# Score products of an attention on 64 by 64 tiles, in a kernel of attention, experts and MLP

## The chip, the core and the metric
The kernel runs on one core of a Trainium2 chip. TensorE (PE) multiplies matrices, and its weight loads (PEld) are listed beside it; VectorE (DVE), ScalarE (ACT) and GpSimd (POOL) work on tiles; SyncE (SP) issues most transfers. The metric is the device time of one execution in microseconds (us), given as the median of several runs.

## What is computed
```python
# q, k, v: (4, 8, 576, 64); p: (4, 8, 32, 64); all float32
def sm_attn(qq, kk, vv):
    s = scale * np.matmul(qq, kk.transpose(0, 1, 3, 2))
    s = s - np.max(s, axis=-1, keepdims=True)
    a = np.exp(s)
    a = a / (np.sum(a, axis=-1, keepdims=True) + 1e-09)
    return np.matmul(a, vv)
p_packed = sm_attn(p, k, v)               # 32 packed queries a head
out = sm_attn(q, p_packed, p_packed)      # 576 tokens attend to the 32 packed rows
...
for e in range(E):                        # _moe_ref: 4 experts, x: (2304, 512)
    h = np.maximum(x @ w1[e], 0.0)        # w1[e]: (512, 1024)
    out += p[:, e:e + 1] * (h @ w2[e])    # w2[e]: (1024, 512)
...
h = x @ w_in                              # _moe2_ref: 512 -> 2048 -> 512
r = np.maximum(h, 0.0)
return ((s * (r * r) + b) @ w_out).astype(np.float32)
```

## The kernel before
The attention works batch by batch (`bi`, four of them). A batch has two groups of four heads (`gi`), and 576 tokens that are cut into two halves of `HT` = 288 (`h`). A head's 64 channels are folded to 32 partitions and two steps `e`, so four heads fill the 128 partitions.

The first score product, `at_s1(bi, gi)` (line 181), multiplies the packed queries of one group, laid out block-diagonally in `pbd` (128 by 128, made by `block_p`), with that group's transposed k (`kqT`, made on VectorE by `trans_kq`, line 152). It makes one PSUM bank a half. `at_exp1` takes the two maxima (L199), the scalar `nm` (L200) and the exponentials (L204). `at_a1t` transposes the result on TensorE in two banks (L216 and L221), `at_pv` (L235) multiplies with v, `at_rs` and `at_pn` (L252 to L272) normalise and write the block-diagonal `sbd`, and `at_pt` (L278) keeps a transposed copy `ptw` that `fold_w1` (L379) multiplies into the experts' first weights. The second score product, `at_s2(bi, gi)` (L289), multiplies `sbd` with the group's transposed q. `at_s2t`, `at_max2`, `at_exp2`, `at_norm2`, `at_a2t` and `at_fin` make the second softmax, and write `a2`, split into a high and a low part.

All these products are plain float32; the trace lists two records for each, with its weight loads beside them. The experts use products of float32r on the split parts: `m1` (L683) makes one block of hidden values, ScalarE writes its high part `hh` (L693) and VectorE its low part `hl` (L694), and `m2` (L711) adds the block into the accumulators. One `m1` and one `m2` are a unit. `advance()` runs `m1` two units ahead of `m2`.

The order of every engine is that of the program (`tc.manual_schedule`). Batch 0 is written out line by line in front of the first unit (the head). Batches 1 to 3 are woven into the units of expert 0: `at(step, fn, ...)` puts an operation in front of unit `step`, and within a step operations run in the order in which they were put there. Batch `n` begins at `s0`, which is 2 for n=1, 16 for n=2 and 32 for n=3. The transpositions of the k of batch n+1 are put at `s0 + 11` to `s0 + 14` of batch n, which is step 16 for the last of batch 2; those of batch 1 at steps 1 and 2. PSUM banks come from `ps_m` (tag "m", two buffers), `ps_h` and, in the head, from the accumulators. Raw k and q share a tag of two buffers ("kq"), transposed k and q another ("kqT").

Of the kernel before, what the change touches and what calls it, by code (L numbers as in the profile page):

```python
# [19 lines left out]
def attention_experts_mlp_kernel(  # L20
# [87 lines left out]
    def load_kq(src, nm, bi, gi):  # L110
        t = att.tile([P, NJ * D], F32, tag="kq", bufs=2, name=f"{nm}{bi}{gi}")
        x = src[bi, 4 * gi : 4 * gi + 4].rearrange("h (r j) d -> (h r) (j d)", j=NJ)
        if bi == 0:
            for c in kq_cuts(nm, bi, gi):
                nc.sync.dma_start(out=t[:, c], in_=x[:, c])
        elif bi % 2 == 0:
            nc.sync.dma_start(out=t, in_=x)
        else:
            for a, z in pairs(bi):
                nc.sync.dma_start(out=t[64 * a : 64 * a + 64], in_=x[64 * z : 64 * z + 64])  # L120
        kq_in[nm, bi, gi] = t

    def load_p(bi):
        x = p[bi].rearrange("(g h) r d -> (h r) g d", g=G)
        t = p_in[:, G * bi : G * bi + G]
        if bi == 0:
            nc.scalar.dma_start(out=t, in_=x)
        elif bi % 2 == 0:
            nc.sync.dma_start(out=t, in_=x)
        else:  # L130
            for a, z in pairs(bi):
                nc.sync.dma_start(out=t[64 * a : 64 * a + 64], in_=x[64 * z : 64 * z + 64])
# [1122 lines left out]
```

## Time and profile before
| | |
|---|---|
| median of 3 runs | 1116.53 us (1115.78 to 1117.95) |
| the profiled execution's own time | 1117.71 us |
| its span, first to last instruction | 1115.9 us |
| TensorE busy | 1097.7 us, 98% |
| VectorE, ScalarE, GpSimd busy | 61%, 36%, 26% |
| first score product, L181, all batches | 64 records, 18.7 us busy |
| second score product, L289 | 64 records, 18.6 us busy |
| fold of w1, L379 | 128 records, 16.0 us busy |

The rows further down are of these views. The stage table gives a stretch, its length, the busy us of PE, PEld, DVE, ACT and POOL (in brackets how many instructions), the granted clock of TensorE as a share of full speed, the share of the DMA engines and GB/s. The chain of waits follows the work that ended last back to what released it. The view in order of time gives start, duration, engine, line, operation, what is written and read, how many instructions were merged, and in brackets how long the engine was idle ahead of it and who released it. Durations of merged matmuls include the pipeline's tail, so a price is better read from start to start.

### The profile page before, as it was taken

Reading aid. Unit: us, or ns where it says so; the run is one execution under the profiler, and the core shown is the slowest. Engines: PE = TensorE matmul, PEld = TensorE weight load, DVE = VectorE, ACT = ScalarE, POOL = GpSimd, SP = SyncE. Lnnn points to the kernel's source line nnn. Section 1 sums busy time; section 2 is a strip of 40 time slices with the busy share of each in tenths; the row PEclk is TensorE's granted clock in tenths of the full one; section 3 lists DMA queues with packets and bytes.
Section 4 is the critical chain, followed back from the end, with each engine's and each line's share of the span. In section 5 each row is a group of like instructions: output and inputs, shape, how many; then the busy total and the mean of one; then the engine's idle time right before and its main releaser. Section 6 shows DMA issues by size and latency. Waiting matters only on the chain.

```text
span 1115.9 us, 18453 instructions
## 1 busy us (share of the span) xinstructions
PE 1097.7 (98%) x7147; PEld 1025.2 (92%) x7147; DVE 685.2 (61%) x1257; ACT 398.9 (36%) x780; POOL 288.9 (26%) x345
## 2 busy tenths in 40 slices
PE   8899999999999999999999999999999999999998
PEld 5788999999999899999999999988999999999996
DVE  6877655467566446556446633569845766675554
ACT  3423222363344343333343322345532332342111
POOL 1421302133322153323263444353211120210000
PEclk9999999999999999999999999999999999999999
DMA  8632331023306685765665641346666565665522
GB/s 260 168 97 65 82 84 58 21 85 97 125 1 198 234 228 148 215 231 162 213 204 153 172 124 67 130 163 229 269 227 208 173 219 183 208 201 191 191 107 85
DMA packets 68999, 175.08 MB, mean 157 GB/s; under 512 B 11440, under 2 KB 28080, under 8 KB 68912
## 3 DMA queue, kind: packets, MB, share of 16 engines
q1 hardware_dynamic: 68064, 172.79, 48.4%
q8 instruction: 56, 0.92, 0.3%
q10 hardware_dynamic: 848, 1.11, 0.3%
q14 instruction: 31, 0.25, 0.1%
HBM read 127.44 MB, written 46.44 MB: 156 GB/s over the span
## 4 chain that ended last, share of the span: by engine, by line
PE 91%; DVE 4%; POOL 1%; issue 1%; DMA 1%; ACT 1%; DVEq 0%; POOLq 0%; ACTq 0%
PE acc L711 35%; PE h L683 18%; PE o L869 17%; PE h L835 15%; PE s L289 1%; PE pp L478 1%; PE s L181 1%; PE pw L379 1%; PE pp L524 1%; PE pv L235 1%; DMA k<-in_k_dram 1%; DVE gg L803 0%; POOL w2l L549 0%; POOL x L737 0%; DVE qT L152 0%
## 5 line engine op out<-in xcount | busy, mean ns | idle before, releaser
L711 PE MATMUL acc<-hl,w2h 128*128 128x288 f32 x1024 | 303.2, 296 | 0.0
L711 PE MATMUL acc<-hh,w2l 128*128 128x288 f32 x1024 | 302.5, 295 | 0.2 <-POOL w2l L549 0.2
L711 PE MATMUL acc<-hh,w2h 128*128 128x288 f32 x1024 | 302.6, 296 | 0.0
L683 PE MATMUL h<-a,w1p 128*128 128x288 f32 x1536 | 252.0, 299 | 2.1 <-DVE hl L694 0.9
L694 DVE SCALAR_TENSOR_TENSOR hl<-h,hh 128x288 fp32r<-128x288 f32 x256 | 116.2, 454 | 189.6 <-ACT hh L693 188.3
L683 PEld LDWEIGHTS h<-a,w1p 128*128 128x128 f32 x1536 | 217.5, 188 | 14.4 <-issue 9.0
L869 PE MATMUL o<-wo,gg 128*128 128x512 f32 x864 | 224.0, 393 | 3.5 <-DVE gg L803 1.9
L835 PE MATMUL h<-xs,wop 128*128 128x384 f32 x1008 | 204.0, 338 | 0.7 <-DVE y L726 0.7
L835 PEld LDWEIGHTS h<-xs,wop 128*128 128x128 f32 x1008 | 180.7, 188 | 13.8 <-DVE y L726 1.4
L711 PEld LDWEIGHTS acc<-hh,w2l 128*128 128x128 f32 x1024 | 192.3, 188 | 0.6 <-POOL w2l L549 0.4
L711 PEld LDWEIGHTS acc<-hl,w2h 128*128 128x128 f32 x1024 | 192.9, 188 | 0.0
L711 PEld LDWEIGHTS acc<-hh,w2h 128*128 128x128 f32 x1024 | 192.7, 188 | 0.0
L869 PEld LDWEIGHTS o<-wo,gg 128*128 128x128 f32 x864 | 160.9, 188 | 27.8 <-DVE gg L803 2.3
L693 ACT ACTIVATE hh<-h 128x288 fp32r<-128x288 f32 x256 | 104.5, 408 | 221.2 <-PE h L683 218.1
L737 POOL TENSOR_TENSOR x<-x,y 128x288 f32<-128x288 f32 (+2 forms) x144 | 88.4, 649 | 161.9 <-DVE y L726 161.7
L789 ACT ACTIVATE yy<-yy 128x768 f32<-128x768 f32 x48 | 40.2, 838 | 113.0 <-DVE yy L855 113.0
L855 DVE TENSOR_TENSOR yy<-h,uv 128x384 f32<-128x384 f32 x96 | 51.1, 553 | 47.5 <-PE h L835 47.4
L549 POOL TENSOR_TENSOR w2l<-w2r,w2h 128x512 fp32r<-128x512 f32 x32 | 41.5, 1298 | 74.8 <-ACT w2h L548 73.2
L799 ACT ACTIVATE gg<-yy,b_sb 128x768 fp32r<-128x768 f32 x48 | 44.8, 934 | 37.3 <-DVE yy L792 36.0
L803 DVE SCALAR_TENSOR_TENSOR gg<-yy,b_sb,gg 128x768 fp32r<-128x768 f32 x48 | 55.7, 1161 | 1.7 <-ACT gg L799 1.7
L792 DVE SCALAR_TENSOR_TENSOR yy<-yy,s_sb 128x768 f32<-128x768 f32 x48 | 51.2, 1068 | 0.0
L660 POOL TENSOR_TENSOR wo<-wo 128x512 fp32r<-128x512 f32 x16 | 23.9, 1502 | 103.7 <-ACT wo L659 103.7
(370 smaller groups left out, 1028.8 us busy)
## 6 DMA issues: line engine op xcount, KB each, us to landing
xs<-xs_dram SPq DMA_DIRECT2D x63, 768.0 KB, 4.3
w1p_dram<-w1o SPq DMA_DIRECT2D x32, 512.0 KB, 3.8
w1p<-w1p_dram SPq DMA_DIRECT2D x128, 128.0 KB, 4.5
xs_dram<-xs SPq DMA_DIRECT2D x21, 768.0 KB, 3.3
w2r<-in_moe_w_dram SPq DMA_DIRECT2D x32, 256.0 KB, 4.1
w1r<-in_moe_w_dram SPq DMA_DIRECT2D x12, 512.0 KB, 4.8
pb<-pn_dram SPq DMA_DIRECT2D x16, 288.0 KB, 4.4
out_dram<-o_sb SPq DMA_DIRECT2D x17, 256.0 KB, 2.0
```

The lines of the kernel that those rows point to most:

```text
L549: nc.gpsimd.tensor_tensor(out=lo, in0=raw, in1=f32(hi), op=ALU.subtract)
L683: nc.tensor.matmul(t[:, :HT], lhsT=w1p_block(e, bi, f, gi, w), rhs=a2[bi][:, x, gi, tok], start=(n == 0), stop=(n == 3 * G - 1),)
L693: nc.scalar.activation(xh, t[:, :HT], AF.Relu)
L694: nc.vector.scalar_tensor_tensor(out=xl, in0=t[:, :HT], scalar=0.0, in1=f32(xh), op0=ALU.max, op1=ALU.subtract)
L711: nc.tensor.matmul(acc[m][:, :HT], lhsT=w[:, col], rhs=x, start=(f == 0 and n == 0), stop=(f == NF - 1 and n == 2),)
L737: nc.gpsimd.tensor_tensor(out=dst, in0=dst, in1=y[:, a - t0 : z - t0], op=ALU.add)
L792: nc.vector.scalar_tensor_tensor(out=y, in0=y, scalar=s_sb, in1=y, op0=ALU.mult, op1=ALU.mult)
L799: nc.scalar.activation(t[:, 0], y, AF.Identity, bias=b_sb)
L803: nc.vector.scalar_tensor_tensor(out=t[:, 1], in0=y, scalar=b_sb, in1=f32(t[:, 0]), op0=ALU.add, op1=ALU.subtract)
L835: nc.tensor.matmul(ps, lhsT=w[:, a, col], rhs=x[:, z, m, :], start=(n == 0), stop=(n == 3 * HK - 1),)
L855: nc.vector.tensor_tensor(out=dst, in0=ps, in1=src, op=ALU.add)
L869: nc.tensor.matmul(o_acc[i], lhsT=lhsT, rhs=w, start=(f == 0 and n == 0), stop=(f == FG - 1 and n == 2),)
```

## The change
Both score products are cut into 64 by 64 tiles. A tile holds two heads, and a call makes one token half `h` for both groups: `at_s1(bi, h)` issues eight products (two `e`, two groups `g`, two head pairs `c`), with `c` choosing the rows and the PSUM bank and `g` the columns and the half of the output's partitions. From there on the first softmax works by head pairs `c` that hold both groups. `at_s2(bi, h)` does the same, with the groups on the rows and the pairs on the output's halves; q is loaded by pairs to match (`load_q`), and the second softmax works by token halves.

The two maxima of a half are taken in a new `at_max1` behind each product. In batches 1 to 3 ScalarE copies the first half's scores to SBUF there, and the exponential reads that copy. In batch 0 a half is a set of nine of every eighteen tokens, so that it needs only the first or the second part of k. `at_exp1` of the second pair moves from step `s0 + 1` to `s0 + 2`. `pbd` and `sbd` shrink to 64 columns, the zeroing of `sbd` goes, and its transposition is one instruction instead of two. Raw k and q have four buffers instead of two; the first loads of k alternate between the groups, the second v is loaded ahead of q. Lines of the weave that put the transpositions of k are not changed. The core of the diff (renamings in the second softmax are left out):

```diff
+    def load_k(bi, gi, cuts=None):
+        if ("k", bi, gi) not in kq_in:
+            kq_in["k", bi, gi] = att.tile([P, NJ * D], F32, tag="kq", bufs=4, name=f"k{bi}{gi}")
+        x = k_src[bi, 4 * gi : 4 * gi + 4].rearrange("h (r j) d -> (h r) (j d)", j=NJ)
+        for c in [slice(None)] if cuts is None else kq_cuts("k", bi)[cuts]:
+            nc.sync.dma_start(out=kq_in["k", bi, gi][:, c], in_=x[:, c])
+    def load_q(bi, c):
+        t = kq_in["q", bi, c] = att.tile([P, NJ * D], F32, tag="kq", bufs=4, name=f"q{bi}{c}")
+        for g in range(G):
+            h = 4 * g + 2 * c
+            nc.sync.dma_start(
+                out=t[64 * g : 64 * g + 64],
+                in_=q_src[bi, h : h + 2].rearrange("h (r j) d -> (h r) (j d)", j=NJ),
+            )
...
-        t = att.tile([P, G, 2, P], F32, tag="pbd", bufs=2, name=f"pbd{bi}")
+        t = att.tile([P, G, 2, 64], F32, tag="pbd", bufs=2, name=f"pbd{bi}")
...
-    def at_s1(bi, gi, tags="mm"):
-        kt = kqT.pop(("k", bi, gi))
-        ps = []
-        for h in range(2):
-            t = bank(f"s1_{bi}{gi}{h}", tags[h])
-            for e in range(2):
-                nc.tensor.matmul(
-                    t[:, :HT],
-                    lhsT=pbd[bi][:, gi, e, :],
-                    rhs=kt[:, e, h * HT : (h + 1) * HT],
-                    start=(e == 0),
-                    stop=(e == 1),
-                )
-            ps.append(t)
-        stt["s1", bi, gi] = ps
-    def at_exp1(bi, gi):
-        ps = stt.pop(("s1", bi, gi))
-        m2 = att.tile([P, 2], F32, tag="m2", bufs=2, name=f"m2_{bi}{gi}")
-        nm = att.tile([P, 1], F32, tag="nm", bufs=2, name=f"nm_{bi}{gi}")
-        s2 = att.tile([P, 2], F32, tag="s2", bufs=2, name=f"s2_{bi}{gi}")
-        rs = att.tile([P, 1], F32, tag="rs", bufs=2, name=f"rs_{bi}{gi}")
-        a1 = att.tile([P, S], F32, tag="a1", bufs=2, name=f"a1_{bi}{gi}")
-        for h in range(2):
-            nc.vector.reduce_max(m2[:, h : h + 1], ps[h][:, :HT], axis=AX.X)
+    def half(x):
+        return slice(64 * x, 64 * x + 64)
+    def at_s1(bi, h, tags="mm"):
+        ps = stt["s1", bi, h] = [bank(f"s1_{bi}{h}{c}", tags[c]) for c in range(2)]
+        for e in range(2):
+            for g in range(G):
+                for c in range(2):
+                    x = kqT["k", bi, g][half(c), e]
+                    t = ps[c][half(g), :HT]
+                    if bi == 0:
+                        x = x.rearrange("a (r j) -> a r j", j=NJ)[:, :, blocks((h,))[0]]
+                        t = t.rearrange("a (r j) -> a r j", r=32)
+                    else:
+                        x = x[:, h * HT : (h + 1) * HT]
+                    nc.tensor.matmul(
+                        t, lhsT=pbd[bi][half(c), g, e, :], rhs=x, start=(e == 0), stop=(e == 1)
+                    )
+    def at_max1(bi, h):
+        for c in range(2):
+            if h == 0:
+                m2 = att.tile([P, 2], F32, tag="m2", bufs=2, name=f"m2_{bi}{c}")
+                a1 = att.tile([P, S], F32, tag="a1", bufs=2, name=f"a1_{bi}{c}")
+                stt["a1", bi, c] = a1, m2
+            a1, m2 = stt["a1", bi, c]
+            ps = stt["s1", bi, h][c][:, :HT]
+            nc.vector.reduce_max(m2[:, h : h + 1], ps, axis=AX.X)
+            if bi and h == 0:
+                nc.scalar.activation(a1[:, :HT], ps, AF.Copy)
+    def at_exp1(bi, c):
+        a1, m2 = stt["a1", bi, c]
+        nm = att.tile([P, 1], F32, tag="nm", bufs=2, name=f"nm_{bi}{c}")
+        s2 = att.tile([P, 2], F32, tag="s2", bufs=2, name=f"s2_{bi}{c}")
+        rs = att.tile([P, 1], F32, tag="rs", bufs=2, name=f"rs_{bi}{c}")
         nc.vector.scalar_tensor_tensor(
             out=nm, in0=m2[:, 0:1], scalar=m2[:, 1:2], in1=nscale, op0=ALU.max, op1=ALU.mult
         )
         for h in range(2):
+            src = stt["s1", bi, h][c][:, :HT]
+            dst = a1[:, h * HT : (h + 1) * HT]
+            if bi == 0:
+                src = src.rearrange("a (r j) -> a r j", r=32)
+                dst = a1.rearrange("a (r j) -> a r j", j=NJ)[:, :, blocks((h,))[0]]
+            elif h == 0:
+                src = dst
             nc.scalar.activation(
-                a1[:, h * HT : (h + 1) * HT], ps[h][:, :HT], AF.Exp,
-                bias=nm, scale=scale, accum_out=s2[:, h : h + 1],
+                dst, src, AF.Exp, bias=nm, scale=scale, accum_out=s2[:, h : h + 1]
             )
-        stt["a1", bi, gi] = (a1, s2, rs)
+        stt["a1", bi, c] = (a1, s2, rs)
...
-        at, vt = stt["a1t", bi, gi], v_in[bi, gi]
+        at = stt["a1t", bi, gi]
...
-                    rhs=vt[:n, z : z + 2, c, :],
+                    rhs=v_in[bi, x][:n, 2 * gi : 2 * gi + 2, c, :],
...
-        sb = att.tile([P, 2, P], F32, tag="sbd", bufs=2, name=f"sbd_{bi}{gi}")
+        sb = att.tile([P, 2, 64], F32, tag="sbd", bufs=2, name=f"sbd_{bi}{gi}")
         nc.gpsimd.memset(pw, 0.0)
-        nc.gpsimd.memset(sb, 0.0)
         stt["pw", bi, gi], stt["sbd", bi, gi] = pw, sb
...
-        pwf = pw.rearrange("a e d -> a (e d)")
-        for c in range(2):
-            r = slice(64 * c, 64 * c + 64)
-            nc.vector.transpose(
-                out=sb[r, :, r].rearrange("a f (e i) -> a e f i", e=2), in_=pwf[r]
-            )
+        nc.vector.transpose(
+            out=sb.rearrange("a f (e i) -> a e f i", e=2), in_=pw.rearrange("a e d -> a (e d)")
+        )
...
-    def at_s2(bi, gi, hs=(0, 1), tag="m"):
-        if 0 in hs:
-            stt["sc", bi, gi] = att.tile([P, NJ, 32], F32, tag="t", bufs=3, name=f"sc_{bi}{gi}")
-        qt, sb = kqT["q", bi, gi], stt["sbd", bi, gi]
-        for h in hs:
-            t = bank(f"s2_{bi}{gi}{h}", tag)
-            for e in range(2):
-                nc.tensor.matmul(
-                    t[:, :HT],
-                    lhsT=sb[:, e, :],
-                    rhs=qt[:, e, h * HT : (h + 1) * HT],
-                    start=(e == 0),
-                    stop=(e == 1),
-                )
-            stt["s2", bi, gi, h] = t
-    def at_s2t(bi, gi, hs=(0, 1)):
-        for h in hs:
+        nc.scalar.activation(
+            ptw[bi][:, :, half(gi ^ bi % 2)], t[:, :P].rearrange("a (g k) -> a g k", g=G), AF.Copy
+        )
+    def at_s2(bi, h, tags="mm"):
+        stt["sc", bi, h] = att.tile([P, NJ, 32], F32, tag="t", bufs=3, name=f"sc_{bi}{h}")
+        ps = [bank(f"s2_{bi}{h}{g}", tags[g]) for g in range(G)]
+        for e in range(2):
+            for c in range(2):
+                for g in range(G):
+                    nc.tensor.matmul(
+                        ps[g][half(c ^ bi % 2), :HT],
+                        lhsT=stt["sbd", bi, c][half(g), e, :],
+                        rhs=kqT["q", bi, c][half(g), e, h * HT : (h + 1) * HT],
+                        start=(e == 0),
+                        stop=(e == 1),
+                    )
+        for g in range(G):
+            stt["s2", bi, h, g] = ps[g]
...
-        for gi in range(G):
-            load_kq(k, "k", 0, gi)
+        for x in range(2):
+            for gi in range(G):
+                load_k(0, gi, slice(x, x + 1))
...
         block_p(0)
-        for gi in range(G):
-            trans_kq("k", 0, gi)
-            load_kq(q, "q", 0, gi)
         load_v(0, 1)
+        for x in range(2):
+            for gi in range(G):
+                trans_kq("k", 0, gi, slice(x, x + 1))
+        for c in range(2):
+            load_q(0, c)
         for c in range(2):
...
         at_s1(0, 0)
         at_s1(0, 1, ("acc0", "acc1"))
+        for h in range(2):
+            at_max1(0, h)
         at_exp1(0, 0)
...
-        at_s2(0, 0, (0,), "acc0")
-        at_s2(0, 1, (0,), "acc1")
+        at_s2(0, 0, ("acc0", "acc1"))
         for gi in range(G):
             at_pt(0, gi, f"acc{2 + gi}")
         fold_w1(0, 0, 0)
+        at_s2(0, 1, ("acc0", "acc1"))
         for gi in range(G):
-            at_s2(0, gi, (1,), f"acc{gi}")
-        for gi in range(G):
-            at_s2t(0, gi, (0,))
-            at_max2(0, gi, (0,), nc.vector)
-            at_exp2(0, gi, (0,))
+            at_s2t(0, 0, (gi,))
+            at_max2(0, 0, (gi,), nc.vector)
+            at_exp2(0, 0, (gi,))
...
             at(1 + gi, trans_kq, "k", 1, gi)
-            at(1 + gi, load_kq, q, "q", 1, gi)
-            at(gi, at_max2, 0, gi, (1,))
-            at(1 + gi, at_exp2, 0, gi, (1,))
-            at(2 + gi, at_norm2, 0, gi, (1,))
-            at(3 + gi, at_a2t, 0, gi, (1,))
-            at(4 + gi, at_fin, 0, gi, (1,), nc.vector)
+            at(1 + gi, load_q, 1, gi)
+            at(gi, at_max2, 0, 1, (gi,))
+            at(1 + gi, at_exp2, 0, 1, (gi,))
+            at(2 + gi, at_norm2, 0, 1, (gi,))
+            at(3 + gi, at_a2t, 0, 1, (gi,))
+            at(4 + gi, at_fin, 0, 1, (gi,), nc.vector)
         for n in range(1, B):
             s0 = (n - 1) * SB + (2 if n == 1 else 0)
             for step, fn, gi in (
-                (0, at_s1, 0), (0, at_exp1, 0), (1, at_s1, 1), (1, at_exp1, 1),
-                (1, at_pz, 0), (1, at_pz, 1), (2, at_a1t, 0), (2, at_rs, 0),
+                (0, at_s1, 0), (0, at_max1, 0), (1, at_s1, 1), (1, at_max1, 1), (1, at_exp1, 0),
+                (1, at_pz, 0), (1, at_pz, 1), (2, at_exp1, 1), (2, at_a1t, 0), (2, at_rs, 0),
                 (3, at_pv, 0), (3, at_pn, 0), (4, at_pt, 0), (4, at_a1t, 1), (4, at_rs, 1),
                 (5, at_pv, 1), (5, at_pn, 1), (6, at_s2, 0), (6, at_s2t, 0), (6, at_max2, 0),
                 (7, at_pt, 1), (7, at_exp2, 0), (8, at_s2, 1), (8, at_s2t, 1), (8, at_max2, 1),
...
```

## Rows read from the trace of the kernel before
**Rows 1.** Stage table, two stretches (columns as named in the section on the profile)
```profile
30.00:60.00 30.00, 27.20 (x192) 23.67 (x193) 26.61 (x52) 12.98 (x35) 12.98 (x20) 1.00 0.62 159
...
92.00:148.00 56.00, 56.00 (x414) 51.27 (x414) 37.49 (x85) 15.61 (x39) 9.85 (x15) 1.00 0.31 80
```

**Rows 2.** Chain of waits that ended last, batch 3: start, us, what
```profile
148.27 1.94 PE s L181 x8
```

**Rows 3.** In order of time, TensorE, around a fold and behind it
```profile
129.50 0.96 PE L683 MATMUL h<-a,w1p 128*128 128x288 f32 x6
...
131.98 1.95 PE L379 MATMUL pw<-w,ptw 128*64 128x256 f32 x16
...
133.86 1.06 PE L683 MATMUL h<-a,w1p 128*128 128x288 f32 x6
...
136.39 0.97 PE L683 MATMUL h<-a,w1p 128*128 128x288 f32 x6
...
138.81 0.97 PE L683 MATMUL h<-a,w1p 128*128 128x288 f32 x6
```

**Rows 4.** The same view, TensorE, batch 2: first score product, four transposes
```profile
93.17 2.10 PE L181 MATMUL s<-kT,pbd 128*128 128x288 f32 x8
...
101.82 0.63 PE L216 MATMUL tr<-ident,a 128*128 128x128 f32 x4
```

**Rows 5.** The same view, VectorE, batch 2
```profile
94.34 1.25 DVE L152 STREAM_TRANSPOSE kT<-k 128x576 f32<-128x576 f32 x1
...
95.42 0.76 DVE L199 TENSOR_REDUCE m<-s 128x1 f32<-128x288 f32 x2
...
96.22 0.22 DVE L200 SCALAR_TENSOR_TENSOR nm<-m,nscale 128x1 f32<-128x1 f32 x1
...
97.88 0.46 DVE L694 SCALAR_TENSOR_TENSOR hl<-h,hh 128x288 fp32r<-128x288 f32 x1 [1.44 <-ACT hh L693]
```

**Rows 6.** The same view, ScalarE, batch 2
```profile
96.47 0.50 ACT L204 ACTIVATE a<-s,nm 128x288 f32<-128x288 f32 x1 [4.26 <-DVE nm L200]
...
97.44 0.41 ACT L693 ACTIVATE hh<-h 128x288 fp32r<-128x288 f32 x1
```

**Rows 7.** The same view, VectorE, batch 1
```profile
40.66 2.29 DVE L152 STREAM_TRANSPOSE kT<-k 128x576 f32<-128x576 f32 x2
...
45.24 0.46 DVE L694 SCALAR_TENSOR_TENSOR hl<-h,hh 128x288 fp32r<-128x288 f32 x1 [1.44 <-ACT hh L693]
...
53.72 1.14 DVE L252 SCALAR_TENSOR_TENSOR rs<-s 128x1 f32<-128x1 f32 x1
```

**Rows 8.** The same view, TensorE, batch 1
```profile
38.97 2.10 PE L181 MATMUL s<-kT,pbd 128*128 128x288 f32 x8
...
50.47 0.75 PE L216 MATMUL tr<-ident,a 128*128 128x128 f32 x4 [1.41 <-ACT a L204]
...
51.08 1.04 PE L683 MATMUL h<-a,w1p 128*128 128x288 f32 x6
...
58.00 0.33 PE L278 MATMUL pt<-ident,pw 128*128 128x128 f32 x1 [0.32 <-DVE pw L268]
```

**Rows 9.** The same view, TensorE, batch 0 and the first m1
```profile
7.05 5.99 PE L181 MATMUL s<-kT,pbd 128*128 128x288 f32 x16 [0.53 <-ACT pbd L163]
...
16.34 2.19 PE L235 MATMUL pv<-v,a1t 128*64 128x128 f32 x28
...
20.65 3.76 PE L289 MATMUL s<-qT,sbd 128*128 128x288 f32 x8 [2.11 <-DVE sbd L272]
...
30.02 1.91 PE L683 MATMUL h<-a,w1p 128*128 128x288 f32 x12 [0.79 <-DVE w1p L394]
```

**Rows 10.** Stage table, one short stretch of the head
```profile
22.00:24.00 2.00, 2.00 (x6) 1.39 (x5) 1.40 (x3) 0.00 (x0) 1.35 (x2) 0.50 1.02 230
```

**Rows 11.** The view in order of time, ScalarE and VectorE, batch 0
```profile
18.84 1.27 ACT L266 ACTIVATE pw<-pv,rs 32x64 f32<-32x64 f32 x4 [1.75 <-DVE rs L255]
...
24.45 0.48 DVE L300 STREAM_TRANSPOSE sc<-s 128x288 f32<-128x288 f32 x1 [0.46 <-PE s L289]
```

More of the change, by code (lines that the diff above doesn't have):

```diff
@@ L99, in attention_experts_mlp_kernel, with kq_cuts @@
     kq_in, kqT, v_in, pbd = {}, {}, {}, {}
-    def pairs(bi):
-        return ((0, 0), (1, 1)) if bi % 2 == 0 else ((0, 1), (1, 0))
-    def kq_cuts(nm, bi, gi):
+    q_src, k_src = q, k
+    def kq_cuts(nm, bi):
         n = 1 if (nm, bi) == ("q", 0) else 2
         return [slice(i * NJ * D // n, (i + 1) * NJ * D // n) for i in range(n)]
[L110 to L121, printed above, removed]
-    def load_p(bi):
[L124 to L132, printed above, removed]
+    def load_k(bi, gi, cuts=None):
[12 more added lines that the diff above has]
+            )
+    def load_p(bi):
+        (nc.sync if bi else nc.scalar).dma_start(
+            out=p_in[:, G * bi : G * bi + G],
+            in_=p[bi].rearrange("(g h) r d -> (h r) g d", g=G),
+        )
     def load_v(bi, gi):
@@ L150, in trans_kq @@
         t, x = kqT[nm, bi, gi], kq_in[nm, bi, gi]
-        for c in kq_cuts(nm, bi, gi)[cuts]:
+        for c in kq_cuts(nm, bi)[cuts]:
             nc.vector.transpose(
@@ L232, in at_pv @@
             for x in range(2):
-                r = slice(64 * x, 64 * x + 64)
-                z = 2 * (x ^ bi % 2)
+                r = half(x)
                 nc.tensor.matmul(
@@ L300, in at_s2t @@
+    def at_s2t(bi, h, gs=(0, 1)):
+        for g in gs:
             nc.vector.transpose(
-                out=stt["sc", bi, gi][:, blocks((h,))[0], :].rearrange("a j i -> a (j i)"),
-                in_=stt.pop(("s2", bi, gi, h))[:, :HT],
-            )
-    def blocks(hs):
-        n = len(hs) * NJ // 2
-        return slice(hs[0] * NJ // 2, hs[0] * NJ // 2 + n), n
-    def at_max2(bi, gi, hs=(0, 1), eng=nc.gpsimd):
-        j, n = blocks(hs)
-        sc = stt["sc", bi, gi][:, j, :]
-        m = att.tile([P, NJ, 1], F32, tag="mx", bufs=2, name=f"mx_{bi}{gi}{hs[0]}")[:, j, :]
+                out=stt["sc", bi, h][:, blocks((g,))[0], :].rearrange("a j i -> a (j i)"),
+                in_=stt.pop(("s2", bi, h, g))[:, :HT],
+            )
@@ L313, in at_max2, with blocks, at_exp2 @@
+    def blocks(gs):
+        n = len(gs) * NJ // 2
+        return slice(gs[0] * NJ // 2, gs[0] * NJ // 2 + n), n
+    def at_max2(bi, h, gs=(0, 1), eng=nc.gpsimd):
+        j, n = blocks(gs)
+        sc = stt["sc", bi, h][:, j, :]
+        m = att.tile([P, NJ, 1], F32, tag="mx", bufs=2, name=f"mx_{bi}{h}{gs[0]}")[:, j, :]
         nc.vector.reduce_max(m.rearrange("a j o -> a (j o)"), sc, axis=AX.X)
         eng.tensor_tensor(out=sc, in0=sc, in1=m.to_broadcast([P, n, 32]), op=ALU.subtract)
-    def at_exp2(bi, gi, hs=(0, 1)):
-        sc = stt["sc", bi, gi][:, blocks(hs)[0], :]
+    def at_exp2(bi, h, gs=(0, 1)):
+        sc = stt["sc", bi, h][:, blocks(gs)[0], :]
@@ L318, in at_exp2, with at_norm2 @@
         nc.scalar.activation(sc, sc, AF.Exp, scale=scale)
-    def at_norm2(bi, gi, hs=(0, 1), eng=nc.gpsimd):
-        j, n = blocks(hs)
-        sc = stt["sc", bi, gi][:, j, :]
-        r = att.tile([P, NJ, 1], F32, tag="r2", bufs=2, name=f"r2_{bi}{gi}{hs[0]}")[:, j, :]
+    def at_norm2(bi, h, gs=(0, 1), eng=nc.gpsimd):
+        j, n = blocks(gs)
+        sc = stt["sc", bi, h][:, j, :]
+        r = att.tile([P, NJ, 1], F32, tag="r2", bufs=2, name=f"r2_{bi}{h}{gs[0]}")[:, j, :]
         rf = r.rearrange("a j o -> a (j o)")
@@ L330, in attention_experts_mlp_kernel, with at_a2t, at_fin @@
     a2 = {}
-    def at_a2t(bi, gi, hs=(0, 1)):
-        j, n = blocks(hs)
-        tag, bufs = ("a1", 2) if hs == (0,) else ("t", 3)
-        t = att.tile([P, S], F32, tag=tag, bufs=bufs, name=f"at_{bi}{gi}{hs[0]}")[:, : n * 32]
-        stt["a2t", bi, gi, hs] = t
+    def at_a2t(bi, h, gs=(0, 1)):
+        j, n = blocks(gs)
+        tag, bufs = ("a1", 2) if (bi, h) == (0, 0) else ("t", 3)
+        t = att.tile([P, S], F32, tag=tag, bufs=bufs, name=f"at_{bi}{h}{gs[0]}")[:, : n * 32]
+        stt["a2t", bi, h, gs] = t
         nc.vector.transpose(
-            out=t, in_=stt["sc", bi, gi][:, j, :].rearrange("a j i -> a (j i)")
+            out=t, in_=stt["sc", bi, h][:, j, :].rearrange("a j i -> a (j i)")
         )
-    def at_fin(bi, gi, hs=(0, 1), eng=nc.gpsimd):
-        j, n = blocks(hs)
-        tok = slice(j.start * 32, j.stop * 32)
+    def at_fin(bi, h, gs=(0, 1), eng=nc.gpsimd):
+        tok = slice(h * HT, (h + 1) * HT)
         if bi not in a2:
             a2[bi] = wa.tile([P, 2, G, S], F32R, tag="a2", bufs=B, name=f"a2_{bi}")
-        t = stt.pop(("a2t", bi, gi, hs))
-        hi, lo = a2[bi][:, 0, gi, tok], a2[bi][:, 1, gi, tok]
+        t = stt.pop(("a2t", bi, h, gs)).rearrange("a (g t) -> a g t", t=HT)
+        hi, lo = (a2[bi][:, x, gs[0] : gs[-1] + 1, tok] for x in range(2))
         nc.scalar.activation(hi, t, AF.Copy)
@@ L990, in attention_experts_mlp_kernel @@
         for gi in range(G):
-            load_kq(k, "k", 1, gi)
+            load_k(1, gi)
             load_v(1, gi)
```

19 lines of the change are left out of this document (10 added, 9 removed).

## The prediction
> **What bounds the kernel now.** I read the stage table first. From 92 to 148 us TensorE is busy for all 56.00 us and VectorE for 37.49; from 30 to 60 us VectorE has 26.61 of 30.00 and TensorE 27.20, with holes [rows 1]. So there are two regimes: up to about 58 us the order of work on VectorE decides, and behind that each microsecond of TensorE counts in full. Next I took the price of one score product from the chain of waits: one call (four fp32 products, eight records of 288 columns) holds the chain for 1.94 us, 0.243 a record [rows 2]. Sixteen such calls exist (first and second product, four batches, two each), so at most 31 us of 1116 can be touched. Twelve lie in the woven part (batches 1 to 3), four in the head (batch 0).
>
> **Price of a tiled call.** A new call has eight products on 64 by 64 tiles, sixteen records of the same 288 columns, in two rounds over four different tiles. If four tiles run at once, that is 16 / 4 x 0.243 = 0.97 us. The trace has no 64 by 64 product with four tiles, but it has the fold of w1, whose 128 by 64 tiles run in pairs: a bare unit step takes 138.81 - 136.39 = 2.42; the step with sixteen fold records takes 133.86 - 129.50 = 4.36, and the next 136.39 - 133.86 = 2.53 [rows 3]. The fold so costs 4.36 + 2.53 - 2 x 2.42 = 2.05. By the column price (256 / 288 x 0.243 = 0.216 a record) eight pairs are 1.73 and sixteen in single file 3.46: pairs do run together, and going into tiles and back costs 2.05 - 1.73 = 0.32. A call after the change is then 0.97 + 0.32 = 1.29, a gain of 0.65. Bounds: no price for the switch gives 0.97 (gain 0.97); pairs only give 1.94 + 0.32 = 2.26 (loss 0.32). I take 1.29, since two column tiles are seen in pairs and the products name four tiles that share neither. Twelve woven calls: 12 x 0.65 = 7.8 us of TensorE work gone, 2.6 a batch.
>
> The Trainium skill (TensorEngine Tiling (Array Packing), Key Properties) says that a change of tiling mode drains TensorE; the 0.32 agrees [rows 3]. The same page's "PSUM Bottleneck" says that tiling speeds up TensorE and not the emptying of PSUM. It speaks against this change: by it the 7.8 are not all kept, as the waits below work out from rows.
>
> **New wait 1: the second transposed scores.** at_a1t takes two banks of the pool with two buffers; the first is the one that held half c=0 of the last score product, the second that of c=1. Before, both exponentials of a group were issued at step s0+1. Now the exponential of c=1 stands at s0+2, on VectorE behind the hl of step s0+1, which waits for ACT's hh, which stands behind the exponential of c=0. From the first record of at_s1(n, 1): products 0.97 and 0.16 until the result (eight records show 2.10 for 1.94 of pace [rows 2, 4]); two maxima to the scalar 0.80, to the exponential 0.25, exponentials to hh 0.97, hh to hl 0.44 [rows 5, 6]; hl 0.46 until the scalar of c=1, then 0.25 and about 1.05 until its bank is free: 5.35 us. TensorE comes to the second transpose after 1.29 + 2.42 + 0.47 (four transposes show 0.63, less the same 0.16 [rows 4]) = 4.18. It waits 1.2 us, in batches 2 and 3; behind it stand the m1 and m2 of that step. The trace shows 0 idle there now.
>
> **New wait 2: the whole k.** at_s1(n, 0) now needs both groups' transposed k. In batch 2 the last transposition is put into step 16, that of at_s1 itself. It runs on VectorE from 94.34 for 1.25, to 95.59 [rows 5]; TensorE begins the product at 93.17 [rows 4]. The wait is 95.59 - 93.17 = 2.4. Batch 3's k is done two steps earlier: nothing.
>
> **Batch 1** is the worst case of both. The transposition of k(1,1) is done at 40.66 + 2.29 = 42.95 [rows 7], and TensorE stands ready at 38.97 [rows 8]. So the product starts at 43.0, the unit's m1 at 44.1, its result is there at 45.1, hh at 45.5, hl at 45.55 instead of 45.24 [rows 7]. From there VectorE's order is the old one and nearly free of gaps, so the scalar of c=1, just ahead of the old rs at 53.72 [rows 7], comes at 54.0, the bank at 54.0 + 0.25 + 1.05 = 55.3, and the m1 behind the transposes at 55.4 instead of 51.08 [rows 8]: 4.3 late. The waits of 1.41 there now, and of the stretch before, are inside that difference. The wait of 0.32 at 58.00 goes [rows 8], since VectorE has time to catch up: 4.0. The two second products give back 1.3. Bounds: 1.0 less or more, by whether the scalar runs in 0.2 us or, like rs now, in 1.14 [rows 7]. Sum +2.7.
>
> **Woven part.** Batch 1 +2.7; batch 2 -2.6 + 2.4 + 1.2 = +1.0; batch 3 -2.6 + 1.2 = -1.4. Together +2.3 us.
>
> **Head.** Work there hangs on VectorE's and ACT's order. Sixteen records of 288 columns take 5.99 from 7.05, the first at half pace [rows 9]; in four-tile rounds the two calls end near 11.1. VectorE then has four maxima and both scalars done by 12.4 and starts on q 1.3 us earlier; q itself is asked for earlier, because four buffers replace two. But the first exponential starts 0.4 later (12.3), as it now stands behind the maxima of both halves, and at_s2(0, 0) needs both groups: pv ends at 16.34 + 2.19 + 0.4 = 18.9 [rows 9], ACT's pn of the second group takes 1.27 [rows 11], one transposition 0.35: 20.6, as now (20.65). Then both halves' results come at once: the second scores' transposition, now at 24.45 [rows 11], comes at 23.0, and VectorE's row of work ends 0.5 earlier. That is the good end, -0.5. The other end is the clock. TensorE now idles from 11.2 to 13.4. The like gap of 2.11 before 20.65 [rows 9] is followed by a granted clock of 0.50 in 22:24, the level of 1.2 GHz [rows 10]. If the new gap does the same, the transposes and pv (2.19 for the last stretch alone [rows 9]) run at half pace: an estimate of 2.4 late at the second product, which is cold as now; two halves at once give 0.2 back: +2.2. I take +1.7, near the cold end, because the new gap is as long as the one that lowered the clock.
>
> **Nothing else.** The memset of sb that goes (at_pz), the halved memset of pbd and the loads by head pairs lie on POOL and SP, which wait there; the ACT copy added per half has ACT idle 4.26 us ahead of it [rows 6]. If that cover were gone, the copies would cost 0.8 a batch on hh. k and q loads issue earlier with four buffers; no wait on SP is added.
>
> **Sum.** +2.3 + 1.7 = +4.0. The profiled execution took 1117.71 (span 1115.9 and 1.8 around it), which gives 1121.7; it lies 1.18 above the median of the three runs, 1116.53, and against that I predict 1120.5 us.
>
> **Rivals.**
> - Head warm, woven waits as worked out: +2.3 - 0.5 = +1.8, 1118.3. For it: TensorE keeps its pace through the half-idle stretch 13 to 18 us today. Against it: rows 10.
> - Faster: the bank is free in time. If the scalar of c=1 gets onto VectorE before the hl (or the transposes get other banks), wait 1 is gone: batches 2 and 3 give 2.4 more, and batch 1 loses only the late start of k (its m1 at 52.0 instead of 51.08: 0.9, less 0.3 and 1.3, -0.7 in place of +2.7). Sum +2.3 - 2.4 - 3.4 = -3.5, with a warm head -4.0: 1112.5. It decides at 4.18 us behind the first record of at_s1(n, 1). Against it: queues run in order, and the code puts hl first.
> - The change doesn't do what it says: four tiles run two at a time. Twelve calls lose 0.97 each against my price, 11.6, part of it inside the waits: about +13, 1130. For it: no row has four tiles at once. Against it: tiles in pairs gave the full factor two.
> - Waits and gains cancel (k's last transposition finds VectorE free sooner, say): within 2 us of now, 1117.
>
> **How the numbers follow.** Forecast 0.50 (own range 1118.5 to 1124.5), warm head 0.17, faster 0.14, pairs only 0.09, cancelling 0.10. 0.2% is 2.2 us and about what a measurement of this kernel can tell from no change. The forecast puts 0.05 of its 0.50 inside that, the warm head 0.11 of its 0.17: same 0.05 + 0.11 + 0.10 = 0.26; faster 0.14; slower 0.60. The range 1113.5 to 1126 leaves out most of the faster case and the pairs.
>
> **What would show it.** Right: sixteen records per score call in about 1.0 us on TensorE; TensorE idle at the second transpose (ACT's exponential as releaser) by about 1.2 in batches 2 and 3 and over 3 in batch 1; idle by about 4 and 2.4 ahead of at_s1(1, 0) and at_s1(2, 0), released by VectorE's k. Wrong: records 0.24 apart one after the other; no idle ahead of those; a first m1, now at 30.02 [rows 9], earlier than 29.

## The result, and the profile after

The changed kernel takes 1126.18 us (median of four, 1124.53 to 1126.22) against 1116.15 for the kernel before in the same comparison: ratio 1.0084, 95% interval 1.0068 to 1.0101, so slower by 0.84% (the ratio is estimated from all runs; the quotient of the two medians is 1.0090). Run again beside the experiments it took 1125.47, ratio 1.0089 (1.0075 to 1.0103). The profiled execution took 1126.21 with a span of 1124.4; before it was 1117.71 and 1115.9, so 8.5 us lie between the two traces.

To see where they lie, I subtracted the start of the same instruction in two traces: the first m2 of a step (an L721 record, L711 before). Shifts are in us against the trace of before; "c0" is the changed kernel once more, the other columns are the experiments below.

| step (its first m2 before) | after | c0 | e1 | e2 | e3 | e4 | e7 | e5 | e6 | e9 |
|---|---|---|---|---|---|---|---|---|---|---|
| 0 (33.77), end of the head | +3.2 | +2.3 | +0.8 | +1.8 | +1.0 | +4.8 | +5.1 | +2.1 | +1.8 | +1.1 |
| 13 (84.08), behind batch 1 | +8.7 | +9.0 | +2.7 | +6.8 | +7.8 | +10.2 | +10.5 | +4.0 | -0.6 | -1.3 |
| 29 (139.62), behind batch 2 | +9.5 | +9.8 | +4.0 | +5.4 | +8.6 | +12.6 | +11.4 | +1.4 | -2.4 | -3.0 |
| 45 (194.49), behind batch 3 | +8.5 | +8.8 | +1.8 | +4.3 | +7.6 | +11.6 | +10.3 | -0.7 | -4.5 | -5.2 |
| span (1115.9) | +8.5 | +7.6 | +1.6 | +4.2 | +6.4 | +10.7 | +10.3 | -0.7 | -4.5 | -6.2 |

There is only one trace of before, and its head had luck of its own: of the sixteen records at L181 [rows 9] the first eight start 0.48 us apart and the other eight 0.24, while after's first product runs at full pace. In another execution the head of before may be up to 8 x 0.24 = 1.9 us earlier (an estimate from these records).

So the changed kernel's trace loses 3.2 in the head, 5.5 in batch 1 and 0.9 in batch 2, and wins 1.0 in batch 3. Behind that its trace loses 1.2 at 482 us (VectorE's wi9e waited 1.9 for its DMA; in c0 this is absent, and its cause was not looked for) and gets 1.2 back at 763 us (754 in the trace of before), in code that was not changed (last section).

The longest waits of TensorE in the trace of after, over the whole span: line, releaser, us in total, times, longest.

```profile
PE tr L235 <- ACT a L219: 6.1, 3, 3.4
PE s L187 <- DVE kT L148: 4.7, 2, 3.0
PE tr L230 <- ACT a L219: 3.0, 2, 2.2
PE h L693 <- DVE w1p L404: 2.7, 1, 2.7
```

The first two are the two waits that were forecast: the fifth transposition of the second scores, one in each woven batch, and the score product that stands for the transposed k, in batches 1 and 2. Of the third, 2.2 lie in the head, and the fourth is the wait ahead of the head's first m1.

The view in order of time, TensorE, batch 2 of after (start, us, engine, line, operation, count, idle before and its releaser). It answers to [rows 4].

```profile
101.27 0.70 PE L187 MATMUL s<-kT,pbd 64*64 64x288 f32 x4
103.69 1.19 PE L187 MATMUL s<-kT,pbd 64*64 64x288 f32 x12 [1.71 <-DVE kT L148]
104.80 1.06 PE L693 MATMUL h<-a,w1p 128*128 128x288 f32 x6
105.70 0.29 PE L721 MATMUL acc<-hh,w2l 128*128 128x288 f32 x1
...
107.41 1.20 PE L187 MATMUL s<-kT,pbd 64*64 64x288 f32 x16
108.54 1.05 PE L693 MATMUL h<-a,w1p 128*128 128x288 f32 x6
109.43 0.29 PE L721 MATMUL acc<-hh,w2l 128*128 128x288 f32 x1
...
111.01 0.63 PE L230 MATMUL tr<-ident,a 128*128 128x128 f32 x4
112.98 0.30 PE L235 MATMUL tr<-ident,a 128*64 128x128 f32 x1 [1.34 <-ACT a L219]
```

The undisturbed call at 107.41 shows the price: sixteen records, and the m1 behind it starts 108.54 - 107.41 = 1.13 later. From m2 to m2 the step takes 109.43 - 105.70 = 3.73. Before, the same step, TensorE:

```profile
95.90 0.29 PE L711 MATMUL acc<-hh,w2l 128*128 128x288 f32 x1
...
97.52 2.10 PE L181 MATMUL s<-kT,pbd 128*128 128x288 f32 x8
99.24 1.16 PE L683 MATMUL h<-a,w1p 128*128 128x288 f32 x6
100.24 0.29 PE L711 MATMUL acc<-hh,w2l 128*128 128x288 f32 x1
```

There the call held TensorE for 99.24 - 97.52 = 1.72, and the step took 4.35: 0.62 won. So the four tiles do run at once: two at a time, sixteen records would take 8 x 0.243 = 1.94. The call at 101.27 does its first four records on the group that is there and then stands for the other. To the m1 it holds TensorE for 104.80 - 101.27 = 3.53, which is 2.40 more than 1.13. At 112.98 the fifth transposition has waited 1.34 for its bank.

Why the bank is late: ScalarE and VectorE in the same stretch.

```profile
111.14 0.46 DVE L704 SCALAR_TENSOR_TENSOR hl<-h,hh 128x288 fp32r<-128x288 f32 x1 [0.36 <-ACT hh L703]
111.52 0.21 DVE L208 SCALAR_TENSOR_TENSOR nm<-m,nscale 128x1 f32<-128x1 f32 x1
...
111.82 0.54 ACT L219 ACTIVATE a<-a,nm 128x288 f32<-128x288 f32 x1 [0.71 <-DVE rs L264]
112.26 0.19 ACT L219 ACTIVATION_READ_ACCUMULATOR a<-a,nm 128x1 f32 x1
112.36 0.48 ACT L219 ACTIVATE a<-s,nm 128x288 f32<-128x288 f32 x1
```

The scalar of c=1 (111.52) stands behind hl on VectorE. Two exponentials follow it on ScalarE: the first reads the copy in SBUF, the second reads the bank and so frees it, at 112.84.

Batch 1 of after, TensorE in order of time (it answers to [rows 8]); behind it two stretches of its stage table, where the last numbers but two are the granted clock.

```profile
42.25 0.70 PE L187 MATMUL s<-kT,pbd 64*64 64x288 f32 x4
45.99 1.92 PE L187 MATMUL s<-kT,pbd 64*64 64x288 f32 x12 [3.04 <-DVE kT L148]
47.84 1.81 PE L693 MATMUL h<-a,w1p 128*128 128x288 f32 x6
...
60.02 0.42 PE L235 MATMUL tr<-ident,a 128*64 128x128 f32 x1 [3.42 <-ACT a L219]
60.10 1.79 PE L693 MATMUL h<-a,w1p 128*128 128x288 f32 x6
61.68 0.44 PE L721 MATMUL acc<-hh,w2l 128*128 128x288 f32 x1
```

```profile
46.00:50.00 4.00, 4.00 (x22) 2.81 (x23) 0.82 (x2) 1.04 (x3) 0.00 (x0) 0.57 0.00 0
...
62.00:64.00 2.00, 2.00 (x12) 1.96 (x11) 1.24 (x2) 1.18 (x3) 1.07 (x1) 0.66 0.00 0
```

Both holes are longer than 3 us. Behind them the granted clock is 0.57 and 0.66 on average, so for most of these stretches at the lower level, 1.2 GHz: the m1 takes 1.81 and 1.79 where it takes 1.05 at 108.54.

### The profile page after: what moved, and what is told of

Same layout as the page of the kernel before. It is cut to its first block, busy times and chain, and to the rows that moved or that the text cites. A ratio compares the mean times of both kernels' runs of the same rounds, so it can differ in the third digit from the quotient of the medians.

```text
span 1124.4 us, 18679 instructions
## 1 busy us (share of the span) xinstructions
PE 1095.1 (97%) x7275; PEld 1013.3 (90%) x7275; DVE 681.7 (61%) x1249; ACT 401.1 (36%) x786; POOL 287.1 (26%) x337
## 4 chain that ended last, share of the span: by engine, by line
PE 90%; DVE 5%; ACT 1%; POOL 1%; issue 1%; DMA 1%; SPq 0%; DVEq 0%; POOLq 0%; ACTq 0%
PE acc L721 35%; PE h L693 18%; PE o L879 17%; PE h L845 15%; PE pp L488 1%; PE pw L389 1%; PE s L299 1%; PE pp L534 1%; PE pv L248 1%; DMA q<-in_q_dram 1%; ACT a L219 1%; PE s L187 1%; DVE kT L148 1%; DVE gg L813 0%; POOL w2l L559 0%
## 5 line engine op out<-in xcount | busy, mean ns | idle before, releaser
L721 PE MATMUL acc<-hh,w2l 128*128 128x288 f32 x1024 | 303.3, 296 | 0.8 <-ACT hh L703 0.6
L721 PE MATMUL acc<-hl,w2h 128*128 128x288 f32 x1024 | 303.4, 296 | 0.0
L721 PE MATMUL acc<-hh,w2h 128*128 128x288 f32 x1024 | 302.9, 296 | 0.0
L721 PEld LDWEIGHTS acc<-hh,w2l 128*128 128x128 f32 x1024 | 192.9, 188 | 1.6 <-ACT hh L703 0.8
L721 PEld LDWEIGHTS acc<-hh,w2h 128*128 128x128 f32 x1024 | 193.3, 189 | 0.0
L721 PEld LDWEIGHTS acc<-hl,w2h 128*128 128x128 f32 x1024 | 193.2, 189 | 0.0
L865 DVE TENSOR_TENSOR uv<-h,uv 128x384 f32<-128x384 f32 x48 | 26.4, 554 | 40.0 <-PE h L845 40.0
```

The source lines that it names most:

```text
L721: nc.tensor.matmul(acc[m][:, :HT], lhsT=w[:, col], rhs=x, start=(f == 0 and n == 0), stop=(f == NF - 1 and n == 2),)
L865: nc.vector.tensor_tensor(out=dst, in0=ps, in1=src, op=ALU.add)
```

## The experiments

The theory under test: the tiles bring what was priced, and the loss comes from three things that were moved with them: the exponential of c=1 (step s0+2), the whole k that a call now needs, and the order of loads in the head; holes in TensorE's work cost more where the clock falls. The rival: VectorE's row of work is the bound, so that a wait taken away in one place comes back in another.

**c0: the changed kernel again**, unedited.

> The changed kernel as it is, to see how far its own head moves from one execution to the next. In two traces of kernels whose head is the same code as the changed kernel's (the exponential moved in the woven part, k transposed earlier in the woven part) the head was 0.75 and 1.75 us behind the kernel before, in the changed kernel's own trace 3.21; and a wait of 1.2 us at 482 us was in that trace alone. If that is spread between executions: a profiled head between 0.7 and 3.5 us late, no wait at 482 us, and a median of 1124 to 1126. If it belongs to the changed kernel: 3.2 us late again, the wait at 482 us again, 1126 us.

Measured 1125.47 (four runs, 1125.30 to 1125.94). The head is 2.3 late instead of 3.2, and the wait at 482 us is not there: both are spread between executions. The shifts by batch are those of the first trace within 1.2 us.

**e1: the exponential of c=1 back at s0+1.**

```diff
-                (0, at_s1, 0), (0, at_max1, 0), (1, at_s1, 1), (1, at_max1, 1), (1, at_exp1, 0),
-                (1, at_pz, 0), (1, at_pz, 1), (2, at_exp1, 1), (2, at_a1t, 0), (2, at_rs, 0),
+                (0, at_s1, 0), (0, at_max1, 0), (1, at_s1, 1), (1, at_max1, 1), (1, at_exp1, 0), (1, at_exp1, 1),
+                (1, at_pz, 0), (1, at_pz, 1), (2, at_a1t, 0), (2, at_rs, 0),
```

> The exponential of c=1 goes back from step s0+2 to step s0+1, ahead of that step's hl on VectorE; nothing else changes. Theory (the second transposed scores wait for a bank that this exponential empties): TensorE's waits ahead of them in the changed kernel, 3.7 us in batch 1, 1.63 in batch 2 and 1.59 in batch 3, go for the most part, about 6 us, so 1118 to 1121 us against 1126.2. Price paid for it: hl and the m2 behind it may come up to 0.8 us later in each of the three batches, which is inside that range. Rival (the bank is not the reason; the time sits in the tiles or in VectorE's total work): the wait only moves to another instruction of the same step and the time stays at 1125 to 1127.

Measured 1118.02 (twelve runs, 1116.93 to 1120.28), ratio 1.0022 (1.0010 to 1.0033). That lies in the expected range, at its fast end. The wait of the fifth transpositions for ScalarE falls from 6.1 in all to 0.6, 0.3 at most; nothing took its place in that step. In batch 2, TensorE:

```profile
97.70 2.13 PE L187 MATMUL s<-kT,pbd 64*64 64x288 f32 x12 [1.71 <-DVE kT L148]
99.76 1.71 PE L693 MATMUL h<-a,w1p 128*128 128x288 f32 x6
...
107.44 0.30 PE L235 MATMUL tr<-ident,a 128*64 128x128 f32 x1 [0.21 <-ACT a L219]
```

The wait for k at 97.70 is as long as in after, 1.71, but here the clock fell behind it: product and m1 take 2.13 and 1.71 instead of 1.19 and 1.06, and from m2 to m2 the step takes 7.70 instead of 6.11. That is the price of the fall alone, 1.6. My expectation for e5, below, took this for a longer wait; it was the clock.

**e2: the next batch's k transposed two steps earlier.**

```diff
-                        at(s0 + 11 + 2 * gi + x, trans_kq, "k", n + 1, gi, slice(x, x + 1))
+                        at(s0 + 9 + 2 * gi + x, trans_kq, "k", n + 1, gi, slice(x, x + 1))
```

> The transpositions of the next batch's k go two steps earlier (s0+9 to s0+12 instead of s0+11 to s0+14); batch 1's k, which is placed elsewhere, stays where it is. Theory (the product at_s1(2,0) stands waiting for the last piece of k): the wait of 2.11 us at 101.6 goes and nothing takes its place, 1124.1 us against 1126.2 (1123.7 to 1124.8). Rival (VectorE is the bound around that step, so that the transpositions only push its other work back): the wait goes, an equal one comes at the m2 of steps 12 to 15, and the time stays within 1 us of 1126.2.

Measured 1122.47 (1121.21 to 1123.76), ratio 1.0066 (1.0049 to 1.0083). The wait in batch 2 is gone: the step that lost 1.76 against before now wins 0.61, a difference of 2.4, and no equal wait appears. That is the forecast mechanism. The time is 1.6 below the expected 1124.1; the head, 1.8 late in this trace and not 3.2, would explain it, but one trace doesn't show that for the median.

**e5: both moves. e6: both, and batch 1's attention one step later.**

```diff
-            s0 = (n - 1) * SB + (2 if n == 1 else 0)
+            s0 = (n - 1) * SB + (3 if n == 1 else 0)
```

> Both moves at once: the exponential of c=1 at s0+1 and the next batch's k two steps earlier. With the exponential alone, batch 2's wait for k grew from 2.1 to about 3.7 us, since TensorE came to the product earlier and VectorE did not. Theory (the two waits are separate, each removed by its own move): the k wait of batch 2 goes whole, 3.3 to 4 us off the time with the exponential alone (1118.0): 1114 to 1115. Rival (VectorE has no room for the transpositions at steps 11 to 14 once TensorE runs ahead): at most 2 us, 1116 or more.

> As with both moves, and batch 1's attention starts one step later (s0 = 3 instead of 2). Theory (TensorE stands about 3.2 us ahead of at_s1(1,0) for the transposed k(1,1), and its granted clock falls to 0.50 in that hole): with another step of about 4 us of expert products ahead of it the wait and the half clock go, nothing else is late, 3 to 4.5 us off: 1110 to 1112, below the kernel before. Rival (VectorE's row of work from 36 to 60 us is the bound, not the one transposition): the wait moves to the second transposes or to the m2 of steps 4 to 6 and less than 1.5 us is gained.

e5: 1116.03 (1114.21 to 1117.04), ratio 0.9997 (0.9987 to 1.0008), so as the kernel before. Less than expected was won on e1 in the median, 2.0, which is the most that the rival allowed. Yet the wait for k is gone from batch 2 and no other took its place, as the theory had it; the two traces differ by 3.8 between step 0 and step 45, of which about 1.6 is the clock that fell in e1's profiled execution. e6: 1112.92 (1110.81 to 1115.90), ratio 0.9971 (0.9959 to 0.9982): faster than both kernels, and 3.1 below e5, as the theory had it (the time itself is 0.9 above the expected range, since e5 was less than hoped for). In batch 1 of e6, TensorE and two stretches of the stage table:

```profile
43.23 0.70 PE L187 MATMUL s<-kT,pbd 64*64 64x288 f32 x4
44.84 1.19 PE L187 MATMUL s<-kT,pbd 64*64 64x288 f32 x12 [0.90 <-DVE kT L148]
45.95 1.05 PE L693 MATMUL h<-a,w1p 128*128 128x288 f32 x6
...
53.24 0.75 PE L230 MATMUL tr<-ident,a 128*128 128x128 f32 x4 [0.91 <-ACT a L219]
54.24 0.30 PE L235 MATMUL tr<-ident,a 128*64 128x128 f32 x1 [0.25 <-ACT a L219]
```

```profile
44.00:50.00 6.00, 5.16 (x48) 3.75 (x49) 4.66 (x14) 1.93 (x5) 2.08 (x3) 1.00 0.31 74
...
58.00:64.00 6.00, 6.00 (x48) 5.59 (x46) 5.82 (x15) 1.85 (x5) 0.16 (x1) 1.00 0.01 3
```

The holes of 3.04 and 3.42 are now 0.90 and 0.25 (0.91 ahead of the four transposes), and the clock stays at 1.00. From step 0 to step 45 e6 wins 6.3 us; twelve calls at 0.61 would be 7.3. TensorE stands idle for 3.7 us in that stretch and for 3.2 in before, so what is won is shorter work and not idle time that went away: nearly all that the tiles bring can be kept. The rival, VectorE as the bound, would have left less than 1.5 to win on e5 and falls. Not run: the same moves in the kernel before, whose batch 1 has holes of its own, 1.41 [rows 8] and 1.05; how much faster the tiles are than the old products in an order that suits those remains open.

**e4 and e7: q's place among the loads.** In e4 both halves of q are issued ahead of both v; in e7 the half c=0 is issued between the two v.

```diff
+        for c in range(2):
+            load_q(0, c)
         load_v(0, 0)
...
-        for c in range(2):
-            load_q(0, c)
```

> The loads of batch 0's q are issued directly behind the first loads of k, ahead of the first v; nothing else changes. Theory Q (q's landing at about 14.5 us sets VectorE's row of work in the head): q's transposition starts 0.8 to 1.5 us earlier and the first m1 by as much, 1124.7 to 1125.4 us against 1126.2. Theory C (the half clock of 12 to 25 us is what costs): the first m1 moves by less than 0.5 us. If v is what comes late in its place, pv waits for it and the time is longer by up to 1 us.

> Against the changed kernel: the first half of batch 0's q (c=0) is issued between the two v instead of behind both. With both q ahead of both v, v landed late (two waits of TensorE, 2.2 us in sum) and the head was 4.8 us behind the kernel before. Theory (the order of the loads in the head decides; v(0,1) is needed later than q of c=0): q's transposition starts at 13 us or earlier instead of 14.5, pv does not wait, the head is within 0.5 to 1.5 us of the kernel before, 1123.5 to 1125. Rival (pv of c=0 already needs both v, so any q ahead of v(0,1) is paid in pv's wait): a wait of pv on v of about 0.5 to 1 us, the head 2 to 4 us late, the time as the changed kernel's or worse.

e4: 1126.91 (1126.03 to 1128.41); e7: 1126.79 (1125.81 to 1127.94). Neither helps: the first theory of each misses. In e4 q's transposition starts 3.1 earlier than in after, but the first m1 1.6 later; in e7 pv waits 2.25 and the head is 5.1 late, more than its rival allowed. After, VectorE in the head; then VectorE and TensorE of e4, and of e7:

```profile
14.54 2.33 DVE L148 STREAM_TRANSPOSE qT<-q 128x1152 f32<-128x1152 f32 x1 [3.37 <-DMA q<-in_q_dram]
```

```profile
11.45 2.33 DVE L148 STREAM_TRANSPOSE qT<-q 128x1152 f32<-128x1152 f32 x1
...
16.32 1.54 PE L248 MATMUL pv<-v,a1t 128*64 128x128 f32 x10 [1.37 <-DMA v<-in_v_dram]
```

```profile
13.79 2.34 DVE L148 STREAM_TRANSPOSE qT<-q 128x1152 f32<-128x1152 f32 x1 [2.46 <-DMA q<-in_q_dram]
...
16.59 1.54 PE L248 MATMUL pv<-v,a1t 128*64 128x128 f32 x10 [2.25 <-DMA v<-in_v_dram]
```

What q gains, v loses: pv of c=0 takes both groups' v, so v(0,1) is needed as early as q. The rival of e7 had the reason right and the size too small. In the kernel before, v(0,1) could come last and nobody waited for it.

**e3 and e9: products in the head's idle places**, in the changed kernel (e3) and in e6 (e9). Each is a 128 by 128 by 512 product of the zeroed tile `warm`, and nobody reads the results.

```diff
         at_s1(0, 1, ("acc0", "acc1"))
+        keep_busy("acc2", 6)
...
+        keep_busy("acc3", 4)
         at_s2(0, 0, ("acc0", "acc1"))
...
         fold_w1(0, 0, 1)
+        keep_busy("acc2", 8)
         fold_hi(0, 0, 1)
```

> Products whose result nobody reads are added in the three places of the head where TensorE stands idle: six behind at_s1(0,1), four ahead of at_s2(0,0), eight ahead of the first fold_hi. Theory C (the head is 3.2 us late mostly because TensorE's granted clock falls to 0.50 in its idle time and the transposes and pv then run at half pace): the granted clock stays at 1 from 12 to 25 us and the first m1 comes 1 to 2 us earlier, 1124 to 1125.2 us against 1126.2. Theory Q (the head is late because q lands late and VectorE's row of work ends later): the clock stays up, but the first m1 and the time stay within 0.5 us of the changed kernel's.

> The three moves (exponential at s0+1, k two steps earlier, batch 1 one step later) together with the products that nobody reads in the three idle places of the head. Theory (with batch 1's holes gone, what is left of the head's lateness is the half clock and VectorE's row): the granted clock stays at 1 from 12 to 22 us, the head comes 0.5 to 1.5 us nearer to that of the kernel before, 1111.5 to 1112.5 us against 1112.9 with the moves alone. Rival (the head ends where VectorE's row of work ends, and q's landing sets that): no difference, 1112.5 to 1113.5.

e3: 1124.88 (1124.04 to 1127.56), ratio 1.0090 (1.0072 to 1.0109) where c0 had 1.0089. The median lies in the range of theory C, but the ratio shows no gain. The same stretch of the stage table in after and in e3, and e3's second product:

```profile
12.00:22.00 10.00, 8.61 (x54) 5.70 (x54) 6.37 (x11) 3.85 (x14) 0.00 (x0) 0.51 1.05 296
```

```profile
12.00:22.00 10.00, 5.98 (x56) 4.08 (x58) 6.53 (x12) 4.08 (x15) 0.00 (x0) 1.00 1.06 293
...
21.85 2.19 PE L299 MATMUL s<-qT,sbd 64*64 64x288 f32 x16 [2.99 <-DVE sbd L281]
```

The clock is at 1.00 instead of 0.51, yet the second product starts at 21.85 (21.32 in after): TensorE stands 2.99 for VectorE, which began q at 15.03 here and at 14.54 in after. So up to the second product the half clock is mostly hidden behind VectorE. e9: 1112.18 (1111.45 to 1114.29), ratio 0.9962 (0.9950 to 0.9975); its interval and that of e6 overlap, so the filling by itself isn't shown to help.

The traces also tell what the head's lateness is made of. Starts in us, and the granted clock between the last two:

| | before | after | c0 | e1 | e2 | e5 | e6 | e3, filled | e9, filled |
|---|---|---|---|---|---|---|---|---|---|
| VectorE begins q | 13.71 | 14.54 | 15.48 | 15.25 | 15.74 | 16.03 | 15.33 | 15.03 | 15.12 |
| second product | 20.65 | 21.32 | 22.10 | 21.87 | 22.37 | 22.68 | 22.42 | 21.85 | 21.64 |
| first m1 | 30.02 | 31.67 | 31.16 | 30.77 | 31.78 | 32.10 | 31.83 | 31.00 | 31.15 |
| first m2 | 33.77 | 36.98 | 36.09 | 34.52 | 35.52 | 35.84 | 35.58 | 34.76 | 34.90 |
| clock, first m1 to first m2 | 1.00 | 0.68 | 0.71 | 1.00 | 1.00 | 1.00 | 1.00 | 1.00 | 1.00 |

VectorE begins q 0.8 to 2.3 late in all of them, and the first m1 comes 0.75 to 2.1 late. From there to the first m2 it is 3.75 wherever the clock stays up, as in before; in after and c0 it fell in or behind the wait ahead of the first m1, for another 1.6 and 1.2. After, and then e1, TensorE:

```profile
31.67 2.58 PE L693 MATMUL h<-a,w1p 128*128 128x288 f32 x12 [2.71 <-DVE w1p L404]
34.18 1.98 PE L389 MATMUL pw<-w,ptw 128*64 128x256 f32 x8
```

```profile
30.77 1.91 PE L693 MATMUL h<-a,w1p 128*128 128x288 f32 x12 [2.11 <-DVE w1p L404]
32.61 1.08 PE L389 MATMUL pw<-w,ptw 128*64 128x256 f32 x8
```

So of the 3.2 of after about half is this fall of the clock. It came in e4 and e7 too (waits of 2.81) and not in the seven traces, before among them, whose wait there was 0.23 to 2.35.

## Why the prediction held, and where its steps did not

It forecast 1120.5, slower, in a range up to 1126.0; the medians are 1126.18 and 1125.47, at its upper end (the first 0.2 above it), and both above the 1124.5 up to which the chosen case was to hold. Forecast was +4.0, measured are 8.7 to 10.0 by the medians. The sign and the two named waits held; two terms were much too small.

- **Price of a call**: forecast 1.29 and a gain of 0.65; measured 1.13 to the next m1, and 0.61 to 0.65 from step to step. The gain is right, the price 0.16 too high; read the same way, from start to the next m1, the old call is 1.72 and not 1.94, so the two errors nearly cancel. The rival "four tiles run two at a time" falls. The Trainium skill (TensorEngine Tiling (Array Packing), PSUM Bottleneck) says that tiling speeds up TensorE and not the emptying of PSUM. The change as it was made lost more than its gain behind late buffers and operands, but e6 keeps 6.3 of 7.3 us, so here most of that loss was in the order of work.
- **New wait 1**, batches 2 and 3: forecast 1.2, measured 1.34 of idle, with the releaser named. From m2 to m2 the step is 1.5 longer than before, and e1 takes 1.1 of it away. Right, and a little small.
- **New wait 2**, batch 2: forecast 2.4, measured 2.40, and e2 removes 2.4. Right. Batch 2 as a whole, +1.0 forecast and +0.9 measured, agrees in part by luck: the step with wait 1 lost 0.3 more than forecast, and a step of before that was 0.6 longer (its m1 waited 0.37 for GpSimd at 86.89) is short again, which the sum didn't have. Batch 3: -1.4 forecast, -1.0 measured, again for the step with wait 1.
- **Batch 1**: forecast +2.7, measured +5.5 and +6.6 (c0). This is the step that failed. The waits are those that were named, but the sum priced the work behind them at full pace: "the unit's m1 at 44.1". Behind each hole the clock fell; a call and m1 of 1.92 + 1.81 stand where 1.19 + 1.06 were assumed, 1.5 more, and the m1 and m2 behind the second hole lose another 1.4. Together 2.9, which is what the sum lacks. VectorE's and ScalarE's row behind the product shows the first part again: from the product (its second piece) to the fifth transposition the sum had 55.3 - 43.0 = 12.3, measured are 60.02 - 45.99 = 14.0. It was no chance of one execution: in all eight traces that have the hole ahead of the product (3.0 to 3.3) the clock falls in it or behind it, and so in all six that have the one ahead of the fifth transposition (3.4). The rise and fall of the clock was weighed for the head alone. e6, with both holes under 1 us, keeps the clock up, and its batch 1 ends ahead of before; what the fall costs apart from the hole shows in batch 2 of e1.
- **Head**: forecast +1.7, measured +3.2, +2.3, and 0.8 to 2.1 in four more traces with the same head: within these traces for a reason that is half wrong. The gap behind the first product (2.20) and the half pace of pv came as forecast, but most of that is hidden, and the second product is 0.7 late in after, not 2.4. What the sum lacked are two other things. "q itself is asked for earlier" is true of its issue (c=0: 5.68 and 6.43 against 6.55) and false of its landing (14.44 against 10.52): 576 KB of v now lie ahead of it, and VectorE waits 3.37 for q where it went from the scalar to q without a wait before. And in after and c0 the clock fell around the first m1, a place that was not weighed (1.6 and 1.2).
- **The rival "faster"** named the right lever: with the scalar of c=1 ahead of hl it gave 1112.5. e1 alone reached 1118.0, since the waits for k cost more than their length (the clock again) and the head was not ahead of before. That e6 comes so near, 1112.9, is luck: it has no wait for k in batch 2, which the rival kept, and a late head, which the rival didn't have.
